# Two thirds of the first batch's up-projections by Strassen's scheme, with pairs of vector instructions joined, in a routed-attention and feed-forward kernel

## The chip, the cores and the metric

The kernel runs on one core of a Trainium2 chip. The metric is the device time of one execution in microseconds; the kernel before takes 1044.93 us, the median of three runs (1044.05 to 1045.06). The profile is of one further execution of 1043.85 us, whose span from the first to the last instruction is 1042.1 us; TensorE's granted clock in it is 0.998 of full speed.

Engines are named as in the profile: PE is TensorE's matmul stream, PEld its weight loads, DVE is VectorE, ACT is ScalarE, POOL is GpSimd, SP is the engine whose queue issues most transfers.

## The reference

Attention over 4 batches, 8 heads, 768 tokens and 64 dimensions per head, in which a query sees only the keys that have the same nearest centroid of 16; then a bilinear feed-forward over the 3072 tokens, 512 wide, 1536 inside:

```python
q_assign = argmax(einsum('bhsd,hcd->bhsc', q_n, c_n))      # k_assign likewise
mask = q_assign[:, :, :, None] == k_assign[:, :, None, :]
scores = where(mask, scale * q @ k.T, -1e9)
attn = exp(scores - max) / (sum + 1e-9)
x = (attn @ v).transpose(0, 2, 1, 3).reshape(3072, 512)
a = x @ w_a;  b = x @ w_b                                  # 512 -> 1536
out = ((a * b) @ w_out).astype(float32)                    # 1536 -> 512
```

The weights w_a, w_b and w_out come as 64-bit floats and are rounded to 32 bits on the chip.

## The kernel before

**The order of the work.** Heads are taken in pairs: 4 pairs a batch, 16 in all. A pair has 6 groups, so a batch has 24 and the kernel 96. In group g TensorE computes the scores of two key blocks (L554), ScalarE takes the exponentials (L563), and TensorE multiplies the probabilities of the group before with v (L596). In between, pieces of the feed-forward of the batch before are taken from a queue, as many as a credit in columns allows:

```python
PER_GROUP = [int(cols / n) + 1 for cols, n in (
    (UP + DOWN * 7 / 8, BG + 5.8), ...)]      # BG = 24 groups a batch
...
if ffn:
    credit += PER_GROUP[...]
    while len(ffn) > least and credit > 0:
        cost, piece = ffn.popleft()
        credit -= cost
        piece()
        if todo:
            todo.popleft()()                  # one step of the preparation
        round_next()                          # one weight part, if due
```

**Weights.** 36 parts of 128 x 512 are loaded, rounded with four VectorE instructions and one GpSimd sum, and then cleared of numbers that are too small ("flush"), with the absolute value taken by ScalarE:

```python
nc.vector.tensor_scalar(out=wi, in0=hi, ...)                    # L280
nc.vector.scalar_tensor_tensor(out=wi, in0=hi, in1=wi, ...)     # L283
nc.vector.tensor_scalar(out=rest, in0=wi, ...)                  # L287
nc.vector.scalar_tensor_tensor(out=rest, in0=lo, in1=rest, ...) # L290
nc.scalar.activation(out=size, in_=upper, func=AF.Abs)          # L294
nc.gpsimd.tensor_tensor(out=w, in0=w, in1=rest, op=ALU.add)     # L295
...
nc.vector.scalar_tensor_tensor(out=w, in0=size, scalar=SMALLEST, in1=w,
                               op0=ALU.is_ge, op1=ALU.mult)     # L302, flush_w
```

Eight parts are rounded in groups 1 to 22, the other 28 from group 23 on, three in two groups.

**Sums and normalization.** The probabilities are summed by one instruction for each of two heads (L585), multiplied with ones on TensorE (L619), inverted by VectorE steps with two 32 x 32 transposes (L639 to L646), and x is multiplied by the inverse (L653), on GpSimd but for one half:

```python
for a in range(2):
    many = p >= HP and (a == 1 or j > 3)
    eng = nc.gpsimd if many else nc.vector
    eng.tensor_tensor(out=acc[:, a, :], in0=..., in1=probs[u][:, a, :], op=ALU.add)
```

**The feed-forward.** Every matmul is issued in two halves of 64 output rows (L679). The first batch's up-projections are plain: for each column block f of 12, each weight and each half of the tokens, four chunks of the 512 inputs. The first half's first 8 pieces start after group 22, when only the first half of x is there:

```python
def up(w_sb, f):
    ps = in_turn()                            # one of three PSUM banks
    for ch in range(NCH):                     # 4
        in_halves(ps[:, 0:HB], w_sb[:, ch, f * P:(f + 1) * P],
                  xTs[b][:, ch, t0:t0 + HB], start=(ch == 0), stop=(ch == NCH - 1))
    return ps
```

The other three batches use Strassen's scheme in Winograd's form: x is cut in quarters (two chunks by half the tokens), a weight into quarters too (two chunks by column blocks i and i + 6), and seven products of two chunks replace eight. Combinations of quarters (S1 to S4 of the weights, T1 to T4 of x) are VectorE subtractions and additions, one instruction for each of the two chunks:

```python
def combine(name, l, r, op):
    for c in range(2):
        nc.vector.tensor_tensor(out=dst[c], in0=l[c], in1=r[c], op=op)   # L783
...
order of products: p1 (11,11)  p2 (12,21)  p6 (S2,T2)  p5 (S1,T1)
                   p7 (S3,T3)  p3 (S4,22)  p4 (22,T4)
```

ScalarE copies a product out of PSUM (L815), VectorE adds the next ones to it (L818), and GpSimd multiplies a by b (L824). The second projection goes by the same scheme in all four batches, with its own combinations (L910, L919).

Of the kernel before, what the change touches and what calls it, by code (L numbers as in the profile page):

```python
# [28 lines left out]
SMALLEST = 1.125 * 2.0 ** -15  # L29

# [5 lines left out]
def kernel(  # L36
# [97 lines left out]
    with tc.If(redo > 0):  # L134
        with ExitStack() as slow:
            long_path(nc, tc, slow, c, q, k, v, out)


def short_path(nc, tc, ctx, c, cn, centroids_in, casts, n_far, q, k, v,
# [32 lines left out]
    sizep = pool("sizep", 2)  # L172
# [96 lines left out]
    flush = []  # L269

    def round_w(i):
        flush_w()
        w = w_parts[i][0]
        wi = w.bitcast(INT32)
        raw = raws.pop(i)
        halves = lambda dt: raw.bitcast(dt).rearrange("p (n two) -> p n two", two=2)
        lo, hi = halves(UINT32)[:, :, 0], halves(INT32)[:, :, 1]


        nc.vector.tensor_scalar(out=wi, in0=hi, scalar1=3, scalar2=0x3FFFFFF8,  # L280
                                op0=ALU.logical_shift_left,
                                op1=ALU.bitwise_and)
        nc.vector.scalar_tensor_tensor(out=wi, in0=hi, scalar=SIGN_TOP, in1=wi,  # L283
                                       op0=ALU.bitwise_and, op1=ALU.bitwise_or)

        rest = wtp.tile([P, WN], FP32, name="rest")
        nc.vector.tensor_scalar(out=rest.bitcast(INT32), in0=wi,  # L287
                                scalar1=SIGN_EXP, scalar2=None,
                                op0=ALU.bitwise_and)
        nc.vector.scalar_tensor_tensor(out=rest, in0=lo, scalar=2.0 ** -52,  # L290
                                       in1=rest, op0=ALU.mult, op1=ALU.mult)

        size = sizep.tile([P, WN], FP32, name="size")
        nc.scalar.activation(out=size, in_=halves(FP32)[:, :, 1], func=AF.Abs)  # L294
        nc.gpsimd.tensor_tensor(out=w, in0=w, in1=rest, op=ALU.add)  # L295
        flush.append((w, size))

    def flush_w():

        while flush:  # L300
            w, size = flush.pop(0)
            nc.vector.scalar_tensor_tensor(out=w, in0=size, scalar=SMALLEST,  # L302
                                           in1=w, op0=ALU.is_ge, op1=ALU.mult)

    stat = zero.tile([P, 4 * NPAIR], FP32, name="stat")
# [151 lines left out]
    def prep_by_blocks(p):  # L457
# [47 lines left out]
        if p == HP:  # L505
            return [[lambda: across(0), lambda: across(1)], [sims_across],
                    assign[:2], assign[2:], [one_hot, one_hot_across], []]
# [3 lines left out]
    def prep_steps(p):  # L511
# [6 lines left out]
        if by_blocks(p):  # L518
            steps = prep_by_blocks(p)
            ready = [lambda s=s: todo.extend(s) for s in steps]  # L520
            ready[1] = both(lambda: prep_sim(p), lambda: load_v(p), steps[1][0],
                            lambda: todo.extend(steps[1][1:]))
            return ready
# [50 lines left out]
    def add_up(u):  # L574
# [5 lines left out]
        acc = accs[p, hf]  # L580
        for a in range(2):

            many = p >= HP and (a == 1 or j > 3)
            eng = nc.gpsimd if many else nc.vector
            eng.tensor_tensor(  # L585
                out=acc[:, a, :],
                in0=probs[u - 1][:, a, :] if j == 1 else acc[:, a, :],
                in1=probs[u][:, a, :], op=ALU.add)
# [39 lines left out]
    def normalize(p, hf):  # L628
# [21 lines left out]
        def apply():  # L650

            eng = nc.vector if (p, hf) == (HP - 1, 0) else nc.gpsimd
            eng.tensor_tensor(out=x, in0=x, in1=den, op=ALU.mult)  # L653
            unchecked.append((4 * p + 2 * hf + 1, inv))

        return [across, invert, back, apply]

    def check_inverses():
        while unchecked:
            n, inv = unchecked.pop()  # L660
            nc.scalar.activation(out=inv, in_=inv, func=AF.Copy,
                                 accum_out=stat[:, n:n + 1])

# [24 lines left out]
    def ffn_block(b, blk):  # L688

        box = {}  # L690
        t0 = blk * HB

        def up(w_sb, f):
            ps = in_turn()
            for ch in range(NCH):
                in_halves(ps[:, 0:HB], w_sb[:, ch, f * P:(f + 1) * P],
                          xTs[b][:, ch, t0:t0 + HB],
# [3 lines left out]
        def piece_a(f):  # L701
            if f == 0:
                box["h"] = hp_.tile([P, NF, HB], FP32, name="h")
            ps = up(wa_sb, f)
            box["a"] = hap.tile([P, HB], FP32, name="ha")
            nc.scalar.copy(out=box["a"], in_=ps[:, 0:HB])

        def piece_b(f):
            ps = up(wb_sb, f)
            nc.vector.tensor_tensor(out=box["h"][:, f, :], in0=box["a"],  # L710
                                    in1=ps[:, 0:HB], op=ALU.mult)

        ups = [(NCH * HB, lambda f=f, piece=piece: piece(f))
               for f in range(NF) for piece in (piece_a, piece_b)]
        return ups, box
# [11 lines left out]
    def room():  # L727
        if not W:
            W["raw"] = [rawp.tile([P, 2 * WN], FP32, name="raw") for _ in range(2)]
            W["size"] = [sizep.tile([P, WN], FP32, name="size") for _ in range(2)]  # L730
            W["comb"] = combp.tile([P, 2 * P], FP32, name="comb")
        return W["raw"], W["size"], W["comb"]
# [4 lines left out]
    def up_room():  # L737
        raw, size, comb = room()
        quarter = lambda t: t[:, 0:2 * HB].rearrange("p (c t) -> p c t", c=2)
        beside = lambda t: t[:, 2 * HB:].rearrange("p (c f) -> p c f", c=2)  # L740
        chunks = lambda t: [t[:, c, :] for c in range(2)]
        W["T3"], W["T2"] = chunks(quarter(raw[0])), chunks(quarter(raw[1]))
        W["T4"] = [t[:, 0:HB] for t in size]
        W["slots"] = [chunks(beside(raw[0])), chunks(beside(raw[1])),
                      chunks(comb.rearrange("p (c f) -> p c f", c=2)),
                      [t[:, HB:] for t in size]]

    def combine_x(b, c):
        if c == 0:
            up_room()  # L750
        x = xTs[b]
        x11, x12 = x[:, c, 0:HB], x[:, c, HB:S]
        x22 = x[:, c + 2, HB:S]
        t2, t3 = W["T2"][c], W["T3"][c]
        for out, l, r in ((t3, x22, x12), (x12, x12, x11), (t2, x22, x12)):
            nc.vector.tensor_tensor(out=out, in0=l, in1=r, op=ALU.subtract)

    def ffn_ups(b, h):

        x = xTs[b]  # L760
        X = {"11": [x[:, c, 0:HB] for c in (0, 1)],
             "T1": [x[:, c, HB:S] for c in (0, 1)],
             "21": [x[:, c, 0:HB] for c in (2, 3)],
             "22": [x[:, c, HB:S] for c in (2, 3)]}

        def combine_t4():
            for c in range(2):
                nc.vector.tensor_tensor(out=W["T4"][c], in0=X["21"][c],
                                        in1=W["T2"][c], op=ALU.subtract)

        def products(w_sb, i, is_a):
            N2 = NF // 2
            A = {m + n: [w_sb[:, c, f * P:(f + 1) * P] for c in cs]
                 for m, f in (("1", i), ("2", i + N2))
                 for n, cs in (("1", (0, 1)), ("2", (2, 3)))}
            box = {}

            def combine(name, l, r, op):
# [3 lines left out]
                for c in range(2):  # L782
                    nc.vector.tensor_tensor(out=dst[c], in0=l[c], in1=r[c], op=op)  # L783
# [16 lines left out]
            def product(name, l, r, start=True):  # L800
                ps = box[name]
                rhs = X[r] if r in X else W[r]
                for c in range(2):
                    in_halves(ps[:, 0:HB], A[l][c], rhs[c],
# [8 lines left out]
            def take(name, k, f):  # L813
                box[name] = place(k, f)
                nc.scalar.copy(out=box[name], in_=box["X"][:, 0:HB])  # L815

# [55 lines left out]
        parts = [products(w_sb, i, w_sb is wa_sb) for i in range(NF // 2)  # L872
                 for w_sb in (wa_sb, wb_sb)]
        pieces = []
        for n, (combinations, ps) in enumerate(parts):
            if n == 0:
                ps[0] = both(*combinations, ps[0])
                ps[2] = both(combine_t4, ps[2])
# [4 lines left out]
        return pieces  # L883
# [9 lines left out]
    def ffn_downs(b, h):  # L893
# [97 lines left out]
        def before():  # L991
            down_room()
# [19 lines left out]
    blocks = {}  # L1012

    def ffn_ready(p, hf):

        b, hp = divmod(p, HP)
        if hp < HP - 1:
            return
        if b > 0:
            if hf == 0:  # L1020
                return
            h = []
            for c in range(2):
                ffn.insert(len(ffn) - FREE_ROOM + c, (0, lambda c=c: combine_x(b, c)))
            ffn.extend(ffn_ups(b, h) + ffn_downs(b, lambda: h))
        elif hf == 0:
            blocks[0] = ffn_block(0, 0)
            ffn.extend(blocks[0][0][0:8])
        else:
            ups0, box0 = blocks[0]  # L1030
            ups, box = ffn_block(0, 1)
            for n in range(3):
                ffn.extend(ups[8 * n:8 * n + 8] + ups0[8 * n + 8:8 * n + 16])
            ffn.extend(ffn_downs(0, lambda: (box0["h"], box["h"])))
# [3 lines left out]
    GPP = UPP // 2  # L1038
# [6 lines left out]
        (UP + DOWN * 7 / 8, BG + 5.8), ((UP + DOWN) * 7 / 8, BG + 0.8),  # L1045
# [7 lines left out]
    for i in range(8, len(w_parts)):  # L1053
        due.setdefault(23 + int((i - 8) / 1.5), []).append(i)
# [34 lines left out]
    for g in range(NG + 3):  # L1089
# [13 lines left out]
        flush_w()  # L1103
# [3 lines left out]
        if g % 3 == late and 0 < g - late:  # L1107
            half = divmod(g // 3 - 1, 2)
            if half == (HP - 1, 1):
                ffn.insert(1, (0, lambda: denominators(HP - 1, 1)))  # L1110
            else:
                denominators(*half)
        if g < NG:
            ready[l]()
        parts = due.get(g, [])

        def round_next():
            if parts:
                i = parts.pop(0)
                round_w(i)  # L1120
                load_w(i + 2)
# [42 lines left out]
    fine = zero.tile([P, 4 * NPAIR], FP32, name="fine")  # L1164
# [15 lines left out]
def long_path(nc, tc, ctx, c, q, k, v, out):  # L1180
# [20 lines left out]
    R = 2 * NC  # L1201

# [200 lines left out]
```

## Time and profile before

| | |
|---|---|
| time, median of 3 | 1044.93 us |
| span of the profiled execution | 1042.1 us |
| VectorE's flush, L302, 36 instructions | 13.2 + 10.9 + 10.7 us |
| VectorE's Strassen combinations, L783, 288 instructions of 128 x 128 | 106.1 us |
| VectorE's sums for two heads, L585, 136 instructions | 88.3 us |
| ScalarE's absolute values, L294, 36 instructions | 24.4 us |
| GpSimd's part of the rounding, L295, 36 instructions | 47.6 us |

How the views are read. The busy table gives for each engine its busy time, its share of the span and its instructions. The chain follows the work that ended last back to its beginning, and names at each step the engine and the line that set the time. A row of the waits names who waited for whom, the total in us, the number of waits and the longest. A row of the timeline has start, length, engine, line, what is written and read, the count, and in brackets the idle time before it with what ended it. A row of the stretches has from:to, its length, the busy time of PE, PEld, DVE, ACT and POOL with their instructions, then TensorE's clock, the transfers' share and GB/s.

A matmul of fp32 data appears as two instructions; counts in the profile are of instructions.

### The profile page before, as it was taken

Reading aid. Unit: us, or ns where it says so; the run is one execution under the profiler, and the core shown is the slowest. Engines: PE = TensorE matmul, PEld = TensorE weight load, DVE = VectorE, ACT = ScalarE, POOL = GpSimd, SP = SyncE. Lnnn points to the kernel's source line nnn. Section 1 sums busy time; section 2 is a strip of 40 time slices with the busy share of each in tenths; the row PEclk is TensorE's granted clock in tenths of the full one; section 3 lists DMA queues with packets and bytes.
Section 4 is the critical chain, followed back from the end, with each engine's and each line's share of the span. In section 5 each row is a group of like instructions: output and inputs, shape, how many; then the busy total and the mean of one; then the engine's idle time right before and its main releaser. Section 6 shows DMA issues by size and latency. Waiting matters only on the chain.

```text
span 1042.1 us, 17904 instructions
## 1 busy us (share of the span) xinstructions
PE 1030.8 (99%) x7158; PEld 500.5 (48%) x7158; DVE 658.7 (63%) x1314; ACT 302.8 (29%) x590; POOL 334.1 (32%) x310
## 2 busy tenths in 40 slices
PE   8999999999999999999999999999999999999997
PEld 5443444444445554444444555444444565444565
DVE  6777888889847447555546746755454835554652
ACT  5665333233322222332323122333232201111100
POOL 1111255555633332343443421444333310211100
PEclk9999999999999999999999999999999999999999
DMA  7334253525220121203020030300000000000001
GB/s 183 87 86 86 70 123 105 127 70 142 63 49 21 30 51 27 35 4 47 5 46 4 23 66 25 46 2 20 1 5 1 12 30 22 1 1 1 3 30 34
DMA packets 120523, 46.49 MB, mean 45 GB/s; under 512 B 106608, under 2 KB 115824, under 8 KB 120432
## 3 DMA queue, kind: packets, MB, share of 16 engines
q1 hardware_dynamic: 120016, 44.85, 18.7%
q8 instruction: 58, 0.95, 0.4%
q10 hardware_dynamic: 416, 0.43, 0.1%
q14 instruction: 33, 0.27, 0.1%
HBM read 37.78 MB, written 6.29 MB: 42 GB/s over the span
## 4 chain that ended last, share of the span: by engine, by line
PE 95%; DVE 2%; issue 1%; POOL 0%; DMA 0%; ACT 0%; DVEq 0%; POOLq 0%
PE m L679 63%; PE s L554 15%; PE O L596 13%; PE s L619 2%; PE m L619 1%; PE s L370 1%; PE m L370 0%; PE m L354 0%; DMA h<-in_q_dram 0%; DVE xT L910 0%; DVE raw L910 0%; PE m L430 0%; POOL xT L653 0%; PE m L384 0%; DVE h L919 0%
## 5 line engine op out<-in xcount | busy, mean ns | idle before, releaser
L563 ACT ACTIVATE pt<-s 128x768 f32<-128x768 f32 x192 | 145.3, 809 | 202.5 <-PE s L554 146.4
L585 POOL TENSOR_TENSOR acc<-acc,pt 128x384 f32<-128x384 f32 x144 | 155.6, 1100 | 60.0 <-ACT pt L563 45.9
L596 PE MATMUL O<-pt,v 128*64 128x384 f32 x768 | 145.1, 499 | 0.0
L554 PE MATMUL s<-qkT 64*128 64x384 f32 x768 | 139.7, 483 | 0.0
L824 POOL TENSOR_TENSOR h<-h,ha 128x384 f32<-128x384 f32 x54 | 56.1, 1041 | 255.6 <-DVE ha L818 255.1
L679 PE MATMUL m<-xT,wb_sb 128*64 128x384 f32 x672 | 116.4, 487 | 0.0
L679 PE MATMUL m<-xT,wa_sb 128*64 128x384 f32 x672 | 116.2, 487 | 0.2 <-DVE xT L653 0.2
L818 DVE TENSOR_TENSOR ha<-ha,m 128x384 f32<-128x384 f32 x72 | 39.6, 551 | 106.5 <-PE m L679 80.4
L815 ACT COPY h<-m 128x384 f32<-128x384 f32 x72 | 34.4, 478 | 184.9 <-PE m L679 184.9
L596 PEld LDWEIGHTS O<-pt,v 128*64 128x64 f32 x768 | 46.7, 136 | 85.7 <-issue 80.0
L679 PE MATMUL m<-wo_sb,h 128*64 128x256 f32 x768 | 86.7, 380 | 0.0
L554 PEld LDWEIGHTS s<-qkT 64*128 64x128 f32 x768 | 70.7, 187 | 31.2 <-issue 0.2
L818 DVE TENSOR_TENSOR h<-h,m 128x384 f32<-128x384 f32 x72 | 39.5, 549 | 72.3 <-PE m L679 46.9
L679 PE MATMUL m<-raw 128*64 128x384 f32 x432 | 78.9, 486 | 0.0
L653 POOL TENSOR_TENSOR xT<-xT,acc 128x384 f32<-128x384 f32 x31 | 32.5, 1048 | 143.2 <-DVE acc L646 143.0
L679 PEld LDWEIGHTS m<-xT,wb_sb 128*64 128x64 f32 x672 | 47.9, 137 | 61.2 <-issue 56.3
L679 PEld LDWEIGHTS m<-xT,wa_sb 128*64 128x64 f32 x672 | 48.0, 137 | 60.4 <-issue 55.6
L679 PEld LDWEIGHTS m<-wo_sb,h 128*64 128x64 f32 x768 | 55.0, 137 | 31.0 <-issue 5.0
L585 DVE TENSOR_TENSOR acc<-acc,pt 128x384 f32<-128x384 f32 x96 | 63.4, 687 | 2.3 <-ACT pt L563 1.0
L679 PE MATMUL m<-xT,h 128*64 128x256 f32 x576 | 64.5, 379 | 0.0
L679 PE MATMUL m<-xT,size 128*64 128x384 f32 x288 | 52.7, 487 | 0.0
L679 PEld LDWEIGHTS m<-xT,h 128*64 128x64 f32 x576 | 41.4, 137 | 22.3 <-issue 2.0
(168 smaller groups left out, 1312.3 us busy)
## 6 DMA issues: line engine op xcount, KB each, us to landing
raw<-in_moe_w_a_dram SPq DMA_DIRECT2D x12, 512.0 KB, 3.9
raw<-in_moe_w_b_dram SPq DMA_DIRECT2D x12, 512.0 KB, 3.6
raw<-in_moe_w_out_dram SPq DMA_DIRECT2D x12, 512.0 KB, 3.7
qk<-in_q_dram SPq DMA_DIRECT2D x48, 96.0 KB, 3.2
qk<-in_k_dram SPq DMA_DIRECT2D x48, 96.0 KB, 3.6
v<-in_v_dram SPq DMA_DIRECT2D x24, 192.0 KB, 3.8
out_dram<-rest SPq DMA_DIRECT2D x24, 128.0 KB, 1.7
v<-in_v_dram SPq DMA_DIRECT2D x4, 384.0 KB, 4.5
```

The source lines that it names most:

```text
L370: nc.tensor.matmul(out=ps[32 * kq:32 * kq + 32, 0:HB], lhsT=cTb[:, hp, :], rhs=qkTs[p][:, kq * HB:(kq + 1) * HB], start=True, stop=True)
L554: nc.tensor.matmul(out=s[:, a, 0:HB], lhsT=Ts[p][r, S + j * P:S + (j + 1) * P], rhs=Ts[p][r, hf * HB:(hf + 1) * HB], start=start, stop=not ...
L563: nc.scalar.activation(out=pt, in_=s[:, :, 0:HB], func=AF.Exp, scale=SCALE)
L585: eng.tensor_tensor(out=acc[:, a, :], in0=probs[u - 1][:, a, :] if j == 1 else acc[:, a, :], in1=probs[u][:, a, :], op=ALU.add)
L596: nc.tensor.matmul(out=O_of[0][a * D:(a + 1) * D, 0:HB], lhsT=vs[p][:, a, j, :], rhs=probs[u][:, a, :], start=(j == 0), stop=(j == NJ - 1))
L619: nc.tensor.matmul(out=ps[a * D:(a + 1) * D, 0:HB], lhsT=ones, rhs=t[:, a, :], start=(n == 0), stop=(n == len(terms) - 1))
L653: eng.tensor_tensor(out=x, in0=x, in1=den, op=ALU.mult)
L679: nc.tensor.matmul(out=ps[half], lhsT=lhsT[:, half], rhs=rhs, **kw)
L815: nc.scalar.copy(out=box[name], in_=box["X"][:, 0:HB])
L818: nc.vector.tensor_tensor(out=box[name], in0=box[name], in1=box[bank][:, 0:HB], op=ALU.add)
L824: nc.gpsimd.tensor_tensor(out=to, in0=to, in1=box[name], op=ALU.mult)
```

## The change

It does eight things:

- Of the first batch's 12 column blocks, the first 8 go by Strassen's scheme, in pairs (0,2), (1,3), (4,6), (5,7); the last 4 stay plain. T1 to T4 lie in the room of the result h that the last 4 blocks fill later.
- A combination takes both chunks in one instruction.
- The first batch's feed-forward starts after group 25, not 22, and some of its combinations are computed in groups 16, 24 and 25, ahead of it. The credit per group is set for the smaller work: (UP x 11/12 + DOWN x 7/8) over BG + 2.8 groups.
- The flush is gone. A weight part is looked at instead: ScalarE takes the absolute value and then a steep Relu whose sum is kept in `stat`; only if some number is too small does the long path at the end, which is otherwise skipped, redo the weights and everything else.
- The transfer of a part is issued after this look, not after the rounding. Rounding resumes at group 26, not 23.
- Sums of the first batch take both heads in one instruction.
- GpSimd applies all inverses. The check of the inverses on ScalarE comes a group later.
- In the fifth pair's preparation, the transpose of the similarities goes into the queue of steps while no feed-forward runs, and the argmax and one-hot steps come a group earlier.

The diff, cut to its core:

```diff
-                for c in range(2):
-                    nc.vector.tensor_tensor(out=dst[c], in0=l[c], in1=r[c], op=op)
+                nc.vector.tensor_tensor(out=dst, in0=l, in1=r, op=op)
...
-            flush.append((w, size))
-    def flush_w(): ...
+        unseen.append((i, halves(FP32)[:, :, 1]))
+    def see_w():
+        while unseen:
+            i, upper = unseen.pop()
+            size = spare()[0].bitcast(BF16)[:, 3 * WN:4 * WN]
+            nc.scalar.activation(out=size, in_=upper, func=AF.Abs)
+            n = 4 * NPAIR + i
+            nc.scalar.activation(out=size, in_=size, func=AF.Relu, scale=-STEEP,
+                                 bias=edge[:, 0:1], accum_out=stat[:, n:n + 1])
+            load_w(i + 2)
...
+        if p < HP:
+            nc.vector.tensor_tensor(out=acc, in0=probs[u - 1] if j == 1 else acc,
+                                    in1=probs[u], op=ALU.add)
+            return
...
         if p == HP:
-            return [[lambda: across(0), lambda: across(1)], [sims_across],
-                    assign[:2], assign[2:], [one_hot, one_hot_across], []]
+            return [[lambda: across(0), lambda: across(1)],
+                    [sims_across] + assign[:2], assign[2:] + [one_hot],
+                    [one_hot_across], [], []]
...
-            ready[1] = both(lambda: prep_sim(p), lambda: load_v(p), steps[1][0],
-                            lambda: todo.extend(steps[1][1:]))
+            ready[1] = both(lambda: prep_sim(p), lambda: load_v(p), lambda: (
+                steps[1].pop(0)() if ffn else None, todo.extend(steps[1])))
...
-            eng = nc.vector if (p, hf) == (HP - 1, 0) else nc.gpsimd
-            eng.tensor_tensor(out=x, in0=x, in1=den, op=ALU.mult)
+            nc.gpsimd.tensor_tensor(out=x, in0=x, in1=den, op=ALU.mult)
...
+        N2, firsts = (NF // 2, range(NF // 2)) if b else (2, (0, 1, 4, 5))
...
+            for n, name in enumerate(("T1", "T2", "T3", "T4")):
+                k, f = divmod(2 * n, 4)
+                W[name] = h[k][:, NF - 4 + f:NF - 2 + f, :]
...
+        last = HP * GPP                                  # 24
+        return {last - 8: lambda: (begin(), combine_x(0, "T1")),
+                last: lambda: [f() for f in combinations[0:2]],   # S1, S2
+                last + 1: lambda: combinations[2]()}              # S3, S4
...
-        elif hf == 0:
-            blocks[0] = ffn_block(0, 0)
-            ffn.extend(blocks[0][0][0:8])
         else:
-            ... (plain pieces of both halves)
+            h = h_first
+            combine_x(0, "T2")
+            ffn.extend(ups_first + plain_ups(0, h, range(NF - 4, NF)))
...
-        (UP + DOWN * 7 / 8, BG + 5.8), ...
+        (UP * 11 / 12 + DOWN * 7 / 8, BG + 2.8), ...
...
-        due.setdefault(23 + int((i - 8) / 1.5), []).append(i)
+        due.setdefault(26 + int((i - 8) / 1.5), []).append(i)
```

## The prediction, made before the change was run

> **What bounds the kernel now.** I read the busy table first, then the chain that ended last, then the stretches, and only then single rows.
>
> The busy table and the chain's shares say where to look:
>
> ```profile
> PE 1030.8 (99%) x7158; PEld 500.5 (48%) x7158; DVE 658.7 (63%) x1314; ACT 302.8 (29%) x590; POOL 334.1 (32%) x310
> ...
> PE 95%; DVE 2%; issue 1%; POOL 0%; DMA 0%; ACT 0%; DVEq 0%; POOLq 0%
> ```
>
> The reader is to see that TensorE is busy for all but 11 us and that 95% of the chain is its work. Busy is not yet "at peak", so the next question is its rate. Three pieces of the chain of waits (start, length, what):
>
> ```profile
> 153.29 5.16 PE m L679 x32
> 158.44 1.72 PE s L554 x12
> 160.17 1.44 PE O L596 x8
> ```
>
> A feed-forward matmul instruction of 384 columns takes 5.16 / 32 = 161 ns; a group of attention takes 1.72 us for its scores and 1.44 us for its weighted sum; nothing lies between the pieces. The chain's last feed-forward piece is 159 us of TensorE without a break. So nearly every microsecond taken out of TensorE's work comes off the time, and nothing else does, except where TensorE waits. The waits of TensorE give only one worth naming:
>
> ```profile
> PE m L619 <- DVE acc L585: 2.1, 1, 2.1
> ```
>
> In order of time it stands just before the first feed-forward, with VectorE's reason a few us earlier:
>
> ```profile
> 95.57 0.58 DVE L478 STREAM_TRANSPOSE sim<-m 128x384 f32<-128x384 f32 x1 [4.66 <-PE m L370]
> ...
> 104.58 1.33 PE L619 MATMUL m<-acc,ones 128*64 128x384 f32 x4 [2.10 <-DVE acc L585]
> ```
>
> VectorE stood 4.66 us at a transpose that needs a TensorE product issued later in the group, then had a weight part to round, a normalization, sums of probabilities, a flush and argmax steps in a row; the sum that the denominators need came late, and TensorE lost 2.1 us.
>
> The stretches (length, then busy time of PE, PEld, DVE, ACT, POOL) show who comes next:
>
> ```profile
> 20.00:95.00 75.00, 75.00 (x506) 34.16 (x501) 58.55 (x107) 47.96 (x87) 13.36 (x11) 1.00 0.35 84
> 140.00:170.00 30.00, 30.00 (x190) 13.16 (x188) 28.25 (x39) 10.09 (x20) 18.87 (x15) 1.00 0.34 97
> 400.00:430.00 30.00, 30.00 (x193) 12.74 (x190) 19.14 (x34) 9.60 (x19) 12.19 (x12) 1.00 0.28 43
> ```
>
> While weights are rounded beside the first feed-forward (140 to 170 us), VectorE is 94% busy and TensorE still does not wait. While a Strassen batch runs with no rounding (400 to 430 us) VectorE is 64% busy. The change puts Strassen into the first stretch: that is the risk.
>
> [...] the flush at L302 takes 680 ns beside an idle GpSimd and 1480 to 1530 beside its sums.
>
> **The change part by part.**
>
> *Matmuls (on the path).* The first batch's up-projections are 12 column blocks x 2 weights x 2 row halves x 4 chunks x 2 output halves = 384 calls, and fp32 makes two instructions of each: 768. As a check, the other three batches have 6 x 2 x 7 products of 8 instructions = 672 each, and 768 + 3 x 672 = 2784 is the sum of the page's 384-column rows at L679. Eight of the twelve blocks now go by Strassen: 4 pairs x 2 weights = 8 sets, each with 7 x 8 = 56 instructions in place of 64. That is 64 fewer, 64 x 161 ns = **-10.3 us**. Nothing else on TensorE changes in count.
>
> *The wait before the feed-forward (on the path).* The transpose that blocked VectorE goes behind the other steps while no feed-forward is there to fill in; the argmax steps come one group earlier; rounding resumes at group 26 and not 23; the sums of two heads are one instruction. I take the 2.1 us as gone, and 0.2 of the wait on xT at 114.3: **-2.3 us**.
>
> *A new wait in its place.* The feed-forward now starts after group 25, and its third product needs T2, which needs the last normalized chunk. Behind group 25's TensorE work lie: similarity transpose 0.58[...], the normalization's 0.57 + 0.22 + 0.58, GpSimd's multiply 1.05 or more[...]. TensorE has 1.72 + 1.44 + two products at 8 x 161 ns = 1.29 each: 5.7 us. It just fits; GpSimd may hold it up: **+0.7 us**.
>
> *VectorE in the Strassen stretch (beside, if it fits).* The credit per group becomes 3725 columns (before 3557), so a group holds 3725 / 768 = 4.85 products, 6.3 us, and with 3.16 of attention and some 0.5 of denominators and similarities it is 9.9 us. In 140 to 260 us (12.5 groups) the rows of VectorE sum to about 108 us. Out go the flush (7 + 6 + 6 at 1.1 us = 21.3) and the plain products' multiplies (7.6): 79 remain. In come Strassen's own rows: in 400 to 560 us the adds and multiplies take 28.4 and the combinations 33.9 per 160 us, which at 4.85 products a group for 5, over 120 us, is about 45[...]. Sum 117 us in 124: **94%**, as high as the old stretch's 94% but with a difference. The plain products need VectorE once in 5.2 us of TensorE; Strassen's need an add in nearly every product, and a bank must be free about two products (2.6 us) after its add. A rounding of 0.42 + 0.69 + 0.43 + 0.69 = 2.2 us in the queue fits into that, two things at once do not. The stretch is 56 products / 4.85 = 11.5 groups, 115 us; I allow for 2% of it: **+2.5 us**, the least certain term.
>
> *Beside other work.* The flush leaves VectorE (36 instructions); ScalarE gets a second pass over each part, about 0.7 us with the read of its accumulator 0.2, 36 x 0.9 = 32 us on an engine 29% busy. [...] GpSimd gets 12 multiplies at 1.04 us. Checks a group later: ScalarE's 15.9 us of waiting for inverses goes, hidden. Start and tail are the same.
>
> *Sum:* 1044.93 - 10.3 - 2.3 + 0.7 + 2.5 = **1035.5 us**.
>
> **Rivals.** First, *VectorE becomes the bound* in the Strassen stretch: for it speak the 94%[...]; against it, that the old stretch ran at the same load with no wait of TensorE, and that the plain third afterwards lets a backlog drain. If VectorE needs 10% more than the stretch has, 8 to 11 us come back and the time is 1041 to 1044. Second, *everything stays hidden*: T2 arrives in time and the stretch runs without a gap; then 1044.93 - 12.6 = 1032.3. Third, *the wait moves*: without early plain products to fill groups 23 to 25, the attention groups there stand alone beside VectorE's combinations, and TensorE could lose 2 to 4 us where it loses 2.1 now; the time would be 1036 to 1038. VectorE's 58.55 of 75 us in the stretch from 20 to 95 us, with no TensorE gap, speaks against it.
>
> **Range and chances.** The middle is 1035.5. The low end is all hidden with half a us of luck in the other small waits, 1031.8; the high end has half of the first rival and the third, 1041. A gain over 2% needs 20.9 us, and work removed and waits together are 12.6: 0.01. Slower by 2% would need new waits of over 30 us: 0.01.
>
> **What would show it.** The 384-column instructions at L679's successor should sum to 2720. TensorE's busy time should fall by about 10 us, and the 2.1 us wait on acc should be gone. A row in which TensorE waits on the T2 subtraction near 110 us shows the new wait; its size tells 0.7 from 4. In the stretch from about 115 to 230 us VectorE should stand near 94%, with few us of TensorE idle, most released by VectorE's adds. If VectorE is full there and TensorE idles over 6 us, the first rival holds. The prediction is wrong if TensorE's rate in that stretch drops without a named wait, or if gaps appear in later batches, where I expect none.

## The result: 1057.26 us, and the profile after

The changed kernel takes 1057.26 us (median of 4 runs, 1055.53 to 1057.62) against 1044.99 us of the kernel before in the same measurement: a ratio of 1.0115, 95% interval 1.0097 to 1.0132. It is 12.3 us slower, where the prediction had it 9.4 us faster.

The busy table (busy us, share of the span, instructions) and the chain's shares by engine, of the changed kernel:

```profile
span 1055.5 us, 17746 instructions
PE 1028.9 (97%) x7094; PEld 496.5 (47%) x7094; DVE 647.0 (61%) x1146; ACT 336.5 (32%) x674; POOL 356.9 (34%) x323
PEclk9999989989999999999999999999999999999999
...
PE 85%; DVE 11%; ACT 1%; issue 1%; POOL 0%; DMA 0%; DVEq 0%; POOLq 0%; ACTq 0%
```

The 64 instructions are gone (7158 to 7094). But TensorE's busy time fell by 1.9 us only, from 1030.8, where 10.3 us of work left; its idle time rose from 11.3 to 26.6 us; VectorE's share of the chain rose from 2 to 11%; and the row of the granted clock, all nines before, has two eights. That is the whole balance of the spans: -10.3 of work, +15.3 of idle time, +8.4 us by which the remaining work took longer, makes +13.4 = 1055.5 - 1042.1.

What TensorE waited for (total us, times, longest):

```profile
PE m L694 <- DVE h L781: 7.2, 1, 7.2
PE m L694 <- DVE ha L836: 4.4, 2, 2.3
PE m L694 <- DVE xT L931: 2.4, 2, 2.0
PE s L563 <- ACT pt L572: 2.0, 6, 0.4
PE m L631 <- DVE acc L591: 1.3, 1, 1.3
```

L781 is the combination of x, L836 the addition of a product in PSUM to the result (L818 before), L931 a combination of w_out (L910 before), L694 the feed-forward's matmuls (L679 before), L591 the sum for two heads in one instruction (L585 before), L631 its multiplication with ones (L619 before), L563 the scores and L572 the exponentials (L554 and L563 before). Three rows of waits on VectorE, of 2.4 to 7.2 us each, are new; the old one on acc shrank from 2.1 to 1.3 us and did not go.

**The first wait.** TensorE in order of time at the first Strassen set, then VectorE in the same time:

```profile
127.36 1.51 PE L694 MATMUL m<-h,pair 128*64 128x384 f32 x8
128.67 1.49 PE L694 MATMUL m<-h,comb 128*64 128x384 f32 x8
137.32 2.83 PE L694 MATMUL m<-h,pair 128*64 128x384 f32 x8 [7.16 <-DVE h L781]
140.08 0.82 PE L563 MATMUL s<-ohT 64*128 64x384 bf16 x4
```

```profile
125.48 1.73 DVE L781 TENSOR_TENSOR h<-xT,h 128x768 f32<-128x768 f32 x1 [1.18 <-POOL xT L663]
127.14 2.01 DVE L597 TENSOR_TENSOR acc<-acc,pt 128x384 f32<-128x384 f32 x2
129.06 0.42 DVE L280 TENSOR_SCALAR wa_sb<-raw 128x512 int32<-128x512 int32 x1
...
131.78 1.25 DVE L280 TENSOR_SCALAR wb_sb<-raw 128x512 int32<-128x512 int32 x1
...
135.39 1.78 DVE L781 TENSOR_TENSOR h<-xT 128x768 f32<-128x768 f32 x1
```

The third product, with T2, starts without a wait: T2 ends at 127.2 us, just in time. The fifth needs T3. T3's operands were there at 125.5 us, but its instruction stands in VectorE's queue behind two sums, two whole weight parts, an argmax step and an addition, and starts at 135.39.

**The clock.** The product after the wait takes 2.83 us for 8 instructions, where the one before it took 1.49. The stretches by 2 us (busy PE, PEld, DVE, ACT, POOL, then the granted clock) show why:

```profile
134.00:136.00 2.00, 0.00 (x0) 0.00 (x0) 1.97 (x4) 0.00 (x0) 0.91 (x1) 0.68 0.18 72
138.00:140.00 2.00, 2.00 (x8) 0.51 (x4) 1.97 (x3) 0.00 (x0) 2.00 (x3) 0.50 0.03 12
142.00:144.00 2.00, 2.00 (x14) 0.77 (x12) 1.97 (x5) 1.70 (x4) 0.24 (x1) 1.00 0.03 8
...
218.00:220.00 2.00, 0.40 (x4) 0.22 (x6) 1.97 (x4) 0.00 (x0) 0.84 (x1) 1.00 0.00 0
226.00:228.00 2.00, 2.00 (x10) 0.72 (x8) 2.00 (x3) 0.00 (x0) 1.92 (x3) 0.50 0.33 62
```

In this long wait the granted clock drops to 0.50 and stays there until some 4 us after work has begun again; at the wait that ends at 219.60 us it drops only when work has begun again. At half clock TensorE was busy from 137.3 to 141.5 us, for 7.9 us between 220 and 230, and for about 3.4 us near 330: work of half that length, so 2.1 + 3.9 + 1.7 = 7.7 us were lost beside the waits. That is nearly all of the 8.4 us by which the work took longer.

**The waits near 220 us** stand in front of the first two products of the seventh Strassen set, with VectorE full. TensorE in order of time, and two stretches of 30 us:

```profile
219.60 2.45 PE L694 MATMUL m<-xT,wa_sb 128*64 128x384 f32 x8 [2.05 <-DVE ha L836]
224.36 2.83 PE L694 MATMUL m<-xT,wa_sb 128*64 128x384 f32 x8 [2.31 <-DVE ha L836]
...
170.00:200.00 30.00, 29.87 (x190) 12.12 (x184) 29.13 (x43) 15.21 (x31) 17.83 (x15) 1.00 0.51 118
200.00:230.00 30.00, 25.64 (x138) 10.29 (x136) 28.46 (x44) 12.03 (x25) 18.75 (x16) 0.83 0.25 80
```

VectorE is 97 and 95% busy. TensorE loses 4.4 us in the two waits, both on VectorE's additions.

### The profile page after: what moved, and what is told of

It reads as the page before. It is cut to its first block, busy times and chain, and to the rows that moved or that the text cites. A ratio compares the mean times of both kernels' runs of the same rounds, so it can differ in the third digit from the quotient of the medians.

```text
span 1055.5 us, 17746 instructions
## 1 busy us (share of the span) xinstructions
PE 1028.9 (97%) x7094; PEld 496.5 (47%) x7094; DVE 647.0 (61%) x1146; ACT 336.5 (32%) x674; POOL 356.9 (34%) x323
## 4 chain that ended last, share of the span: by engine, by line
PE 85%; DVE 11%; ACT 1%; issue 1%; POOL 0%; DMA 0%; DVEq 0%; POOLq 0%; ACTq 0%
PE m L694 57%; PE s L563 13%; PE O L608 11%; PE s L631 1%; PE m L631 1%; DVE pair L800 1%; PE s L378 1%; DVE acc L597 1%; DVE acc L591 1%; DVE xT L931 1%; DVE rest L287 1%; ACT pt L572 1%; PE m L378 1%; DVE wa_sb L283 0%; DVE wa_sb L280 0%
## 5 line engine op out<-in xcount | busy, mean ns | idle before, releaser
L572 ACT ACTIVATE pt<-s 128x768 f32<-128x768 f32 x192 | 145.3, 807 | 191.1 <-PE s L563 149.1
L842 POOL TENSOR_TENSOR h<-h,ha 128x384 f32<-128x384 f32 x66 | 71.8, 1095 | 258.2 <-DVE ha L836 256.4
L563 PE MATMUL s<-qkT 64*128 64x384 f32 x768 | 141.3, 487 | 0.0
L836 DVE TENSOR_TENSOR ha<-ha,m 128x384 f32<-128x384 f32 x88 | 48.1, 549 | 115.6 <-PE m L694 90.1
L832 ACT COPY h<-m 128x384 f32<-128x384 f32 x88 | 42.2, 479 | 220.0 <-PE m L694 220.0
L836 DVE TENSOR_TENSOR h<-h,m 128x384 f32<-128x384 f32 x88 | 48.1, 547 | 87.3 <-PE m L694 60.8
L694 PE MATMUL m<-xT,wa_sb 128*64 128x384 f32 x480 | 85.8, 498 | 4.6 <-DVE ha L836 4.4
L694 PE MATMUL m<-wo_sb,h 128*64 128x256 f32 x768 | 86.7, 379 | 0.0
L563 PEld LDWEIGHTS s<-qkT 64*128 64x128 f32 x768 | 71.5, 190 | 32.0 <-issue 1.4
L694 PE MATMUL m<-xT,wb_sb 128*64 128x384 f32 x480 | 83.1, 486 | 0.0
L694 PE MATMUL m<-raw 128*64 128x384 f32 x432 | 78.8, 486 | 0.0
L694 PEld LDWEIGHTS m<-wo_sb,h 128*64 128x64 f32 x768 | 55.1, 137 | 30.1 <-issue 3.7
L694 PE MATMUL m<-xT,h 128*64 128x256 f32 x576 | 66.3, 386 | 2.4 <-DVE xT L931 2.4
L694 PE MATMUL m<-xT,pair 128*64 128x384 f32 x352 | 64.4, 487 | 0.0
L832 ACT COPY ha<-m 128x384 f32<-128x384 f32 x66 | 31.6, 478 | 97.4 <-PE m L694 97.4
L694 PEld LDWEIGHTS m<-xT,wa_sb 128*64 128x64 f32 x480 | 34.2, 139 | 50.3 <-issue 36.5
L694 PEld LDWEIGHTS m<-xT,wb_sb 128*64 128x64 f32 x480 | 34.4, 137 | 43.1 <-issue 38.4
L694 PEld LDWEIGHTS m<-xT,h 128*64 128x64 f32 x576 | 41.8, 139 | 25.8 <-DVE xT L931 3.5
```

Source lines behind the costliest of these rows:

```text
L563: nc.tensor.matmul(out=s[:, a, 0:HB], lhsT=Ts[p][r, S + j * P:S + (j + 1) * P], rhs=Ts[p][r, hf * HB:(hf + 1) * HB], start=start, stop=not ...
L572: nc.scalar.activation(out=pt, in_=s[:, :, 0:HB], func=AF.Exp, scale=SCALE)
L694: nc.tensor.matmul(out=ps[half], lhsT=lhsT[:, half], rhs=rhs, **kw)
L836: nc.vector.tensor_tensor(out=box[name], in0=box[name], in1=box[bank][:, 0:HB], op=ALU.add)
L842: nc.gpsimd.tensor_tensor(out=to, in0=to, in1=box[name], op=ALU.mult)
```

## The experiments

The theory after these readings had three parts. **A**: T3's place in VectorE's queue makes the first wait. **B**: VectorE's load, with Strassen and the rounding in one stretch, makes the others, and will move them about if only the order changes. **C**: each wait costs more than its length, because the clock is halved after it. The rivals: other parts of the change (ScalarE's second pass, the late start, GpSimd's inverses) are to blame; or the half clock costs nothing, as TensorE waits for VectorE anyway. Each run's kernel is the changed one with the edit shown; ratios are to the kernel before, measured beside it.

### T3 earlier

```diff
-                ps[1] = both(ps[1], lambda: combine_x(b, "T3"))
...
             combine_x(0, "T2")
+            combine_x(0, "T3")
```

> T3 of the first batch is computed directly behind T2, in front of the two weight parts of group 26, and nothing else changes. Theory A (the 7.2 us wait is T3's place in VectorE's queue, and the clock that TensorE loses after it goes with it): that wait goes, and with it about 2 us of half clock; the adds that still stand behind the two parts let TensorE wait 1 to 3 us two products later. Time 1048 to 1051 us. Rival B (VectorE is simply full, and any order moves the wait elsewhere): the wait comes back whole within group 27, and the time stays within 2 us of 1057.

Measured: 1055.88 us (1051.42 to 1056.22), ratio 1.0095 (1.0069 to 1.0121). The 7.2 us wait is gone, and this came instead:

```profile
136.51 1.51 PE L694 MATMUL m<-xT,pair 128*64 128x384 f32 x8 [1.80 <-DVE h L836]
140.83 1.51 PE L694 MATMUL m<-h,wa_sb 128*64 128x384 f32 x8 [2.81 <-DVE h L781]
145.63 2.77 PE L694 MATMUL m<-xT,wb_sb 128*64 128x384 f32 x8 [1.99 <-DVE h L836]
```

1.80 + 2.81 + 1.99 = 6.6 us: the first addition, T4 and the next addition stood behind the same two parts. So A is right about T3 and says little about the time, which missed the expected 1048 to 1051; the queue as a whole was late. The first spell of half clock now begins at 145.7 us, after the third of these waits.

### Less rounding work

The correction by the low word is left out for parts 8 to 35 (the output is then less exact in the weights):

```diff
-        rest = wtp.tile(...)            # L287, L290 on VectorE, L292 on GpSimd
+        if i < 8:
+            rest = wtp.tile(...)
```

> Leaves out the correction by the low word for weight parts 8 to 35: two of VectorE's four instructions (about 1.1 us a part) and GpSimd's sum (1.3 us a part). Theory B (VectorE's load in the Strassen stretch makes the waits near 217 and 222 us, 4.4 us, and the half clock after them some 4 us more): these go whole, the T3 wait falls from 7.2 to about 4.5 us, the wait of the second projection near 328 us shrinks to about 1 us; time 1043 to 1047 us. Rival (the waits come from the order of the queue or from ScalarE's second pass, not from VectorE's load): the waits near 217 and 222 us stay, and the time is above 1052 us.

Measured: 1043.16 us (1041.97 to 1043.85), ratio 0.9987 (0.9980 to 0.9993). The stretches of this run:

```profile
140.00:170.00 30.00, 30.00 (x190) 13.11 (x188) 19.98 (x36) 14.60 (x30) 9.18 (x9) 1.00 0.24 75
200.00:230.00 30.00, 30.00 (x189) 12.85 (x187) 21.15 (x38) 15.40 (x32) 11.22 (x11) 1.00 0.28 84
```

VectorE falls to 67 and 71%, TensorE has no gap there, and the wait on the second projection is 0.2 us. T3's wait is still 5.1 us, with a clock of 0.88 in the stretch from 112 to 140 us, as its place in the queue is unchanged. Of the 14.1 us gained, ScalarE's second pass has no part: it is the same. So the rounding beside Strassen makes these waits, as B has it. What this run does not part is VectorE's load from the order of its queue, as a shorter part also holds up less of what stands behind it, nor from GpSimd's sums, which went with it.

### The first batch plain

```diff
-        if g in early:
-            todo.append(early[g])
...
-            combine_x(0, "T2")
-            ffn.extend(ups_first + plain_ups(0, h, range(NF - 4, NF)))
+            h.extend(hp_.tile([P, NF, HB], FP32, name="h") for _ in range(2))
+            ffn.extend(plain_ups(0, h, range(NF)))
...
-        (UP * 11 / 12 + DOWN * 7 / 8, BG + 2.8), ...
+        (UP + DOWN * 7 / 8, BG + 2.8), ...
```

> All twelve column blocks of the first batch's up-projections plain again, without early combinations, all else of the change kept; 64 matmul instructions of 161 ns (10.3 us) come back. Theory B: without Strassen's adds and combinations beside the rounding VectorE has room, no wait over 1 us between 112 and 320 us and a clock of 1.00 there; a wait of up to 2.4 us near 330 us may stay; time 1043 to 1048 us, below the changed kernel though TensorE has more to do. Rival (the loss comes from the other parts of the change: ScalarE's second pass, the late start, GpSimd's inverses): the waits stay and the time is 1057 to 1068 us.

Measured: 1044.99 us (1044.53 to 1045.71), ratio 1.0004 (0.9995 to 1.0012). With 10.3 us more of matmuls it is 12.3 us below the changed kernel. No wait of TensorE is named between 110 and 320 us, and the clock is 1.00. So all the other parts of the change together move the time by nothing that this measures, and the loss comes with Strassen in the first batch, beside the rounding.

### Filling the waits with useless work

This asks for the price of the half clock. Products of the identity with itself are issued where TensorE waited, into columns 384 to 511 of a PSUM bank, which nothing reads. In a first form they were transposes into the feed-forward's own bank:

> TensorE gets useless transposes in front of the products that wait: 28 in the T3 wait (about 6.7 us), 8 and 13 in the two waits near 217 and 222 us, 8 in the wait near 328 us; some 13.6 us of work more, nothing taken away. Theory C (TensorE's clock is halved after a wait of about 2 us or more, and this costs some 7 to 8 us on top of the waits): the clock stays at 1.00 in these places and the time FALLS, to 1050 to 1053 us. Rival (the half clock costs nothing, because TensorE waits for VectorE anyway, or the clock falls for another reason): 1057 to 1059 us.

Measured: 1070.96 us, ratio 1.0253 (1.0235 to 1.0270). It answers nothing. The transposes go into a bank in use, and the output is off by 0.31 (relative error); they also had to wait for VectorE themselves (8.4 us near 226 and 7.6 us near 339 us in its trace), and 28 of them took only 3.3 us. The second form goes to the bank of the weighted sums, continuing its accumulation:

```diff
+    def fill(n):
+        for _ in range(n):
+            nc.tensor.matmul(out=O_of[0][:, HB:512], lhsT=ident, rhs=ident,
+                             start=False, stop=False, skip_group_check=True)
...
+            if b == 0 and n == 0:                       # first Strassen set
+                ps[4] = both(lambda: fill(30), ps[4])
+            if b == 0 and n == 6:
+                ps[0] = both(lambda: fill(8), ps[0])
+                ps[1] = both(lambda: fill(14), ps[1])
...
+            if b == 0 and n == 0:                       # second projection
+                ps[2] = both(lambda: fill(8), ps[2])
```

> The same question as with the transposes before, whose bank made them wait themselves: useless products of the identity with itself go into unused columns of the bank of the weighted sums, which nothing else reads, so that they need not wait: 30 in the T3 wait (some 7 us), 8 and 14 in the two waits near 217 and 222 us, 8 in the wait near 328 us; some 14 us of TensorE's work more, nothing taken away. Theory C (the clock is halved after a wait of about 2 us or more, and that costs some 7 us beside the waits): clock 1.00 in these places, and the time FALLS by 3 to 7 us against the changed kernel's 1057.3, to 1050 to 1054 us. Rival (the half clock is hidden behind VectorE): 1057 to 1060 us.

Measured: 1053.07 us (1051.99 to 1053.36), ratio 1.0078 (1.0061 to 1.0095), mean clock 1.000. Two of the stretches above in this run, which stands 1.6 us later at 130 us and level with the trace above at 219.6 us:

```profile
138.00:140.00 2.00, 1.73 (x14) 1.10 (x13) 2.00 (x2) 0.00 (x0) 2.00 (x3) 1.00 0.71 242
226.00:228.00 2.00, 2.00 (x16) 1.01 (x14) 2.00 (x3) 0.98 (x2) 1.92 (x3) 1.00 0.31 53
```

VectorE is as full as before (2.00 of 2.00), TensorE has 120 instructions more, and the time falls by 4.2 us. Nothing else was taken away, so the half clock cost at least that: C is shown. From the start of T3's wait to the end this trace is 6.0 us shorter than the one above, as it reaches that point 1.6 us later. Some of the 7.7 us was not gained, as TensorE waits for VectorE either way: in steps of 2 us from 218 to 230 us VectorE is busy for 1.97, 1.97, 1.86, 2.00, 2.00 and 1.93 us in both traces.

### Rounding moved, in five forms

The first form starts it one group later and changes nothing else:

```diff
-        due.setdefault(26 + int((i - 8) / 1.5), []).append(i)
+        due.setdefault(27 + int((i - 8) / 1.6), []).append(i)
```

> Rounding of parts 8 to 35 starts at group 27 and not 26, at 1.6 a group and not 1.5; nothing else. Theory A (the two parts in front of T3 make its wait): T3's wait falls from 7.2 us to under 2 us, with the half clock after it. Theory B (VectorE is full over the whole stretch): the time saved comes back as longer waits within the next groups and near 217 us, and the time is 1052 to 1058 us. If A alone were enough: 1047 to 1049 us.

Measured: 1052.41 us (1051.09 to 1054.30), ratio 1.0074 (1.0058 to 1.0091). T3's wait is 1.1 us. But 3.4 us appear at 155 and 0.8 + 3.7 us near 214 to 221 us, with a granted clock of 0.73 from 150 to 160 us and 0.69 from 220 to 230, and of the 8 us that A alone would give, 4.9 are left. Again A is right in its place, and B takes much of it back.

The second form takes a part of the load away as well, with T3 early: 12 parts in groups 1, 3, ... 23, the others from 27 on at 1.4 a group.

> Twelve weight parts, not eight, are rounded before the feed-forward (one every two groups), the other 24 from group 27 on at 1.4 a group and not 1.5 from 26; and T3 directly behind T2. Theory B (VectorE's load beside Strassen): with some 10 us of rounding taken out of the stretch and none in group 26, the waits there fall from 11.6 us to under 3 us with one half-clock spell at most; time 1033 to 1040 us. Rival (VectorE stays full, because GpSimd holds it up): waits of 6 us and more remain in the stretch, time above 1045 us.

Measured: 1045.57 us (1042.95 to 1047.45), ratio 1.0001 (0.9992 to 1.0010). Nearly 12 us are gone, but the expected 1033 to 1040 was missed. TensorE waited 1.9 us at 112 us for the one-hot transfer, as the part of group 23 delayed those steps, and 4.8 us in three waits on VectorE's additions, the longest 2.1, with TensorE idle for 4.1 us between 210 and 220 us. The granted clock was 0.83 from 110 to 120 us, 0.69 from 210 to 220 and 0.79 from 220 to 230.

The third and fourth forms put the load where the profile has room: 11 parts by group 21, 13 in groups 27 to 36, 12 beside the plain products in groups 37 to 43; once with T3 early and once without.

```diff
+    due = {2 * i + 1: [i] for i in range(11)}
+    for i in range(11, len(w_parts)):
+        due.setdefault(27 + int((i - 11) / 1.25) if i < 24 else
+                       37 + int((i - 24) / 1.8), []).append(i)
```

> VectorE's rounding is laid where VectorE has room: 11 parts before the feed-forward (one every two groups, to group 21), 13 in groups 27 to 36 beside Strassen (1.25 a group), 12 in groups 37 to 43 beside the plain products (1.8 a group); T3 directly behind T2. Theory B with the queue (VectorE's load beside Strassen sets the waits): at about 1.25 x 2.6 us of rounding a group in place of 1.5 x 2.6, VectorE falls from 96 to some 85 to 90% there, the waits between 112 and 340 us fall under 3 us in sum with no spell of half clock, and the time is 1033 to 1037 us, below both kernels. Rival (GpSimd's sums hold VectorE up whatever the order, so that waits of over 4 us and a slow spell stay): 1042 us or more.

> The same schedule of the rounding, with T3 left in its place behind the second product. Theory A and B together: with no part in group 26, T3's place costs a wait of 1 to 2 us only, without a slow spell; time 1034 to 1038 us. If T3's place mattered by itself: a wait of over 4 us before the fifth product, time above 1040 us.

Measured with T3 early: 1042.19 us (1040.22 to 1043.55), ratio 0.9973 (0.9965 to 0.9982); without: 1042.90 us (1040.90 to 1044.76), ratio 0.9981 (0.9972 to 0.9990). Both beat the kernel before, by 0.2 to 0.3%, and both missed the expected 1033 to 1038. The first time lies in the range given to the rival (GpSimd's sums hold VectorE up); the last form speaks against that rival. T3's place costs 1.1 us of wait here and no more. What stayed was 2.9 us in group 31, where two parts were due and VectorE had stood 3.05 us at a similarity transpose before, and about 2 us at group 24.

The last form follows from that: never two parts in a group beside Strassen until group 36, and none in groups 18 to 26.

```diff
+    due = {g: [i] for i, g in enumerate((1, 2, 3, 5, 6, 7, 9, 11, 12, 13, 15, 17))}
+    due.update({27 + n: [12 + n] for n in range(9)})
+    due.update({36: [21, 22], 37: [23, 24]})
+    due.update({38 + n: [25 + 2 * n, 26 + 2 * n] for n in range(5)})
+    due[43] = [35]
```

> As the schedule before with T3 early, but never two parts in one group beside Strassen until group 36: 12 parts by group 17 (so none stands in front of the fifth pair's one-hot steps), one a group in groups 27 to 35, two in each of 36 to 42. The waits left by the schedule before were 2.1 us on the one-hot transfer at group 24, 2.9 us in a group with two parts, and 1.2 us in two smaller ones. Theory B in its sharp form (a wait arises where two parts, or one part and the argmax steps, stand in VectorE's queue in front of the add that frees a bank): these go but for under 1.5 us, no spell of half clock, time 1034 to 1038 us. Rival (the mean load of VectorE decides, and it is the same as before): the waits move to other groups, 1040 to 1043 us.

Measured: **1036.52 us** (1036.17 to 1036.97), ratio 0.9920 (0.9906 to 0.9933): 8.8 us below the kernel before and 20.7 below the changed one, with the same number of instructions on every engine. GpSimd has as much to do as in the changed kernel (362.9 us against 356.9), so its sums alone do not make the waits. Its busy table, its two largest waits of TensorE, its two stretches, and its fifth product:

```profile
PE 1021.4 (99%) x7094; PEld 495.5 (48%) x7094; DVE 652.4 (63%) x1146; ACT 335.9 (32%) x674; POOL 362.9 (35%) x323
...
PE m L631 <- DVE acc L591: 3.4, 5, 1.3
PE O L1094 <- DVE ones L84: 1.1, 1, 1.1
...
170.00:200.00 30.00, 30.00 (x192) 12.65 (x190) 26.08 (x41) 13.71 (x28) 16.45 (x14) 1.00 0.43 101
200.00:230.00 30.00, 30.00 (x188) 12.85 (x184) 27.10 (x43) 14.76 (x30) 17.20 (x15) 1.00 0.19 55
...
130.10 1.49 PE L694 MATMUL m<-h,pair 128*64 128x384 f32 x8
```

TensorE's busy time is 9.4 us below the kernel before's, so Strassen's 10.3 us are all but there. VectorE stands at 87 and 90% beside Strassen, and TensorE has no gap in these stretches. Of the waits on acc, 3.4 us in five, the changed kernel has 1.3 as well; the other 2.1 came with the denser rounding of the first groups. ScalarE's six waits are gone with it.

How far the load and how far the order did this is not fully parted. Between the two last forms VectorE's mean load beside Strassen is 92% (69.0 of 75 us from 140 to 215) against 88% (53.0 of 60 us from 140 to 200), and the number of parts that meet in one group changed too.

## Why the prediction was wrong, point by point

**The matmuls, -10.3 us: right.** The 384-column rows of the feed-forward sum to 2720 instructions, and where nothing waits TensorE's busy time falls by 9.4 us (last form).

**The wait before the feed-forward, -2.3 us: wrong size.** The wait on acc went from 2.1 to 1.3 us only, and six waits of TensorE on the exponentials came, 2.0 us in sum, in the first batch. In those groups ScalarE's second pass, which the prediction had put down as hidden "on an engine 29% busy", stands in the queue in front of the exponentials. No run takes this pass away alone; the runs that round in other groups before the feed-forward have none of these waits. The 0.2 us on xT went as expected, so the term was about +1.0.

**"A new wait in its place", +0.7 us: the wrong instruction.** The step followed T2, and "just fits", an estimate, came out right: T2 took 1.73 us and ended in time. But T3, written behind the second product, comes in the queue behind everything that group 26 gives VectorE, two weight parts among it. The step looked at the data T3 needs, and not at its place in the queue. It measured 7.2 us, and 2.1 of half clock.

**VectorE in the Strassen stretch, +2.5 us: the load right, its price wrong.** The working gave 94%; the trace has 27.24 + 29.13 + 28.46 = 84.8 of 90 us from 140 to 230, which is 94%. What joining two combinations saves was an estimate there; measured, 288 instructions of 128 x 128 took 106.1 us before (368 ns each, 737 a pair), and the changed kernel's 176 of 128 x 256 at L800 take 105.3 us (598 ns each). What failed is the allowance of 2% for it. In queue order with two parts in a group, that load made waits of 4.4 us, 2.4 more at the second projection, which no step had looked at, and 3.9 + 1.7 us of half clock: 12.4 in place of 2.5. The step itself said that a bank must be free two products after its add and that two things at once in the queue would not fit; it did not look up how often there would be two, although the list of due parts says so. The old stretch carried 94% with no wait, so the percentage was never the test.

**What no step had: the clock.** TensorE's work was priced everywhere at 161 ns an instruction, as traced in the kernel before; whether it can go faster was not shown. At half clock it was slower (2.83 us for 8 instructions after the first wait, 1.49 before it), and 7.7 us of the result are this. The prediction named a falling rate only as something that would make it wrong "without a named wait"; it came with the waits. In the trace of the changed kernel the granted clock is 0.50 in three spells: 6.83 us from 134.7, 10.24 us from 220.0 and 3.41 us from 329.3. The first begins within the wait of 7.16 us; some 2 us of waiting came before the others: 2.05 us up to 219.60 and 2.03 us up to 328.13.

The sum by terms measured in the traces: -10.3 + 1.0 + 9.3 + 12.4 = +12.4, against +13.4 between the two traces (+12.3 between the medians); 1.0 us is left without a cause.

**The rivals.** The first, VectorE as the bound, was the right one: named with 8 to 11 us and a time of 1041 to 1044, it came with more, for the clock. The third, a wait that moves, was half right: the waits moved behind group 25, not into groups 23 to 25. The second is what the last form comes close to: 1036.5 against its 1032.3.

## What to carry to other kernels

When work is moved onto a stretch whose second engine is near full, list that engine's queue in issue order for the fullest group and follow each operand to its place in it; a load in per cent says neither that it fits nor that it does not. An instruction whose data are ready waits for all that stands in front of it (T3's were there at 125.5 us, and it started at 135.39), and chores with no deadline, such as the rounding here, belong where that engine has room and singly. On TensorE price a wait of about 2 us or more higher than its length: in the changed kernel spells of 3.41 to 10.24 us at half clock came with such waits, though in other runs waits of 2.2 and 2.9 us cost no clock.

## What the runs showed of the hardware that was not expected

Useless work can save time: 120 instructions more on TensorE, in its waits, took 4.2 us off, because the clock stayed at 1.00. And not every wait of 2 us halves the clock. With 2.05 us before the scores of group 24 the schedule with T3 early kept 1.00; with 1.99 us at the same place the one without fell to 0.83 in the mean from 110 to 120 us. A wait of 2.2 us near 325 us of the kernel that rounds from group 27 cost no clock (1.00 from 322 to 332 us), and one of 2.05 us near 219 us of the changed kernel did (0.50 from 220.0 us).

A wait of 2.9 us in group 31 parts the same two schedules. The stretches of 10 us around both places, first without T3 early, then with it:

```profile
110.00:120.00 10.00, 8.01 (x40) 4.08 (x38) 7.64 (x11) 3.80 (x7) 2.67 (x2) 0.83 0.32 72
180.00:190.00 10.00, 7.09 (x46) 2.70 (x40) 8.99 (x14) 4.20 (x10) 4.04 (x4) 0.98 0.62 130
190.00:200.00 10.00, 10.00 (x56) 4.22 (x52) 8.39 (x14) 3.87 (x7) 6.51 (x7) 0.85 0.26 86
...
110.00:120.00 10.00, 7.95 (x51) 3.66 (x48) 7.16 (x10) 4.21 (x10) 2.93 (x2) 1.00 0.33 62
180.00:190.00 10.00, 7.09 (x46) 2.96 (x44) 9.82 (x14) 4.32 (x9) 6.80 (x6) 1.00 0.54 145
190.00:200.00 10.00, 10.00 (x64) 4.34 (x62) 9.79 (x16) 4.54 (x9) 6.34 (x6) 1.00 0.19 54
```

TensorE is idle for about 2.0 and 2.9 us in both, and the clock falls in one only. So the length of a wait alone does not decide it; what does is not shown, as no run moved a wait on purpose. The scatter of kernels with such waits goes with it: with T3 early alone, one run took 1051.42 us at a mean clock of 0.999 and the other three 1055.59 to 1056.22 us at 0.993 or 0.994. The last form, whose waits are all under 1.4 us, stays within 0.8.
